# Gate products of the first expert in one timed sequence, and a shorter pause in the gate scaling

## The chip, the cores and the metric

One core of a Trainium2 chip runs the whole program. The metric is the device time of one launch in microseconds (us); lower is better. The core has five engines, each of which takes its instructions strictly in the order in which they are written for it: PE multiplies matrices, DVE (vector), ACT (scalar) and POOL (GpSimd) work on arrays, and SP here only issues DMAs. An engine whose next instruction waits for a semaphore does nothing else meanwhile, even if later instructions could run.

## The reference

Three stages follow one another: an attention with exponential features, a feed-forward layer with squared ReLU, and a mixture of 8 experts over 2304 tokens of width 512. Only the last one concerns us:

```python
logits = x @ w_gate
P = np.exp(logits - logits.max())
for _ in range(8):
    P /= P.sum(1, keepdims=True) + 1e-09
    P /= P.sum(0, keepdims=True) + 1e-09
    P *= N / E
for e in range(E):
    h = np.maximum(x @ w1[e], 0.0)
    out += P[:, e:e + 1] * (h @ w2[e])
```

Every token passes through every expert; `P[:, e]`, the gate of expert e, weighs its result. The eight rounds of scaling need the logits of all tokens, so no gate exists before they are done.

## The kernel before

The expert stage is cut into 16 passes (8 experts, two halves of 512 hidden columns each), and each pass into three groups of 768 tokens, which the code calls pairs (two blocks of 384). The index `n` runs over the 48 combinations; n = 0 to 2 are the first half of expert 0 on pairs 0, 1 and 2, n = 3 to 5 its second half, and n = 6 begins expert 1.

For each n there are two layers, `layer1(n)` and `layer2(n)`. Each is a fast matrix product that does with 7 products (`p1` to `p7` in `SLOTS`) what would take 8 blocks. One such product is 12 matmuls of 128x384. All operands are kept as a high and a low part: ACT casts the high part (L912), DVE subtracts it from the value to get the low part (L913). The results of layer 1 become the operands of layer 2 in `hidden_forms`: POOL forms four differences t1 to t4 (L1205), ACT and DVE split them and three plain blocks. Layer 2 adds its products into `accT` (L1293).

The loop at L1379 interleaves `layer2(n)` with `layer1(n + 1)`, one product of each per step, seven steps per n. Work that fits nowhere in particular is a list of generators, `side`; `tick()` lets the first of them make one move. There are two ticks per step, so 14 per n, and 7 more while `layer1(0)` runs alone. The gate scaling `sinkhorn()` is the first such generator: after the logits it makes `WAIT` empty moves, then eight rounds of four moves, and then puts the gates into DRAM (`prT`, L1159). By the code's count it uses 60 ticks, the last of them the eleventh tick of n = 3.

A gate reaches SBUF by `load_gate` (L1164): 768 gates, repeated on 128 partitions, into one of two buffers of the name `gate`. From expert 1 on it is applied inside layer 1 (L1245). Expert 0 starts before any gate exists, so its sum is multiplied later: `gate_first(q)` loads the gates of pair q and after eight moves multiplies the four rows of `accT` of that pair (L1323), with an empty move after each.

The code's order is not the order on the engines. All instructions pass through a scheduler that runs a model of the program in time and writes down, for each engine, a fixed order; `tc.issue_after` only says what may not come earlier. The expert stage stays on PE in names as follows: `psa` and `psb` are accumulators, `xh` holds weights, `xl` and `hv` the split operands, `w2v` weights of layer 2. The three partial sums that ACT takes out of an accumulator between products (`ma`, `my`, `mu`, L1192) get the next products added by DVE (L1252).

Of the kernel before, what the change touches and what calls it, by code (L numbers as in the profile page):

```python
# [20 lines left out]
def tile_features_attention__moe__sinkhorn_moe(  # L21
# [18 lines left out]
    nc = tc.nc  # L40
# [5 lines left out]
    NE, _, FE = w1.shape  # L46
    KD = DM // P
# [94 lines left out]
    N1 = len(passes)  # L142
    NJ = FE // FB
# [36 lines left out]
    def fetch(p):  # L180

        if p >= NP:
            return
        if p >= N1:
            for w in range(2):
                wf[p, w] = stage(p, w)
                nc.sync.dma_start(wf[p, w], passes[p][w].rearrange("(k p) f -> p k f", p=P))
                yield
            return
        order = [(w, i) for w in range(2) for i in range(KD)]  # L190
        load_raw(p, *order[0])
        for j, (w, i) in enumerate(order):
            if j + 1 < len(order):
                load_raw(p, *order[j + 1])
            decode(p, w, i)
            yield
# [18 lines left out]
    latest = {}  # L215
# [13 lines left out]
    def layer1(p, f, t0, n):  # L229
        wh, wl = wsp[p, 0]  # L230
        ps = pmm.tile([P, 512], F32, tag="mm", name="ps1")
        cs = slice(f * P, (f + 1) * P)
        for kk in range(KD):
            mm3(
                ps[:, :n], wh[:, kk, cs], wl[:, kk, cs],
                xh[:, kk, t0 : t0 + n], xl[:, kk, t0 : t0 + n],
                kk == 0, kk == KD - 1,
            )
        return ps
# [24 lines left out]
    def first_l1(pool, t0, n, fs=range(NFT)):  # L264
        return [split_square(pool, layer1(0, f, t0, n), n, HALF) for f in fs]
# [574 lines left out]
    accT = acc.rearrange("p t d -> p (t d)").rearrange("p (k n) -> p k n", k=KD)  # L840
# [3 lines left out]
    with tc.tile_pool(name="hp1t", bufs=1, reuse_waits="tile") as hpt:  # L844
        g = [ahead + first_l1(hp, *halves[-2], range(len(ahead), NFT)), first_l1(hpt, *halves[-1])]
# [17 lines left out]
    side = []  # L863

    def tick():
        while side:
            try:
                next(side[0])
                return
            except StopIteration:  # L870
                side.pop(0)
# [27 lines left out]


    NB = 384
    WAIT = 20
    NPR = NT // (2 * NB)
    KH = KD // 2
    SLOTS = (("a", "p1", "b11"), ("b", "p5", "t1"), ("a", "p6", "t2"), ("b", "p3", "b22"), ("a", "p7", "t3"), ("b", "p2", "b21"), ("a", "p4", "t4"))
# [70 lines left out]
    order = [(p, q) for p in range(N1, NP) for q in range(NPR)]  # L976

    def split_forms(p, w, dst, temp):

        f = wf.pop((p, w))  # L980

        def a(i, k):
            return f[:, KH * (k - 1) : KH * k, FH * (i - 1) : FH * i]

        s1, s2 = temp(), temp()
        nc.gpsimd.tensor_tensor(s1, a(2, 1), a(2, 2), ALU.add)  # L986
        nc.gpsimd.tensor_tensor(s2, s1, a(1, 1), ALU.subtract)
        nc.gpsimd.tensor_tensor(a(2, 1), a(1, 1), a(2, 1), ALU.subtract)
        of = {"p1": a(1, 1), "p5": s1, "p6": s2, "p3": s2, "p7": a(2, 1), "p2": a(1, 2), "p4": a(2, 2)}
        for i, (_, nm, _) in enumerate(SLOTS):  # L990
            if nm == "p3":
                nc.gpsimd.tensor_tensor(s2, a(1, 2), s2, ALU.subtract)
            split_form(of[nm], dst[i])
            yield
# [57 lines left out]
    for p in range(1, N1):  # L1052
# [10 lines left out]
        for bi, (t0, n) in enumerate(blocks):  # L1063
            g = []
# [46 lines left out]
    def sinkhorn():  # L1111
# [18 lines left out]

        for _ in range(WAIT):
            yield
# [29 lines left out]
    def load_gate(e, q):  # L1162
        g = hp.tile([P, 2, NB], F32, tag="gate", bufs=2, name="gate")
        nc.sync.dma_start(  # L1164
            g.rearrange("p a (t n) -> p (a t) n", n=P),
            prT[2 * NB // P * q : 2 * NB // P * (q + 1), e : e + 1].rearrange("t e n -> e t n").to_broadcast([P, 2 * NB // P, P]),
        )
        return g
# [28 lines left out]
    def hidden_forms(n):  # L1197

        r = hid[n]["r"]
        out = hid[n]["v"] = {}  # L1200
        t = {}

        def diff(nm, x, y):
            t[nm] = sum_tile(nm)
            nc.gpsimd.tensor_tensor(t[nm], x, y, ALU.subtract)  # L1205

        def form(nm, src):
            out[nm] = form_tile()
            split_form(src, out[nm])

        diff("t1", r["12"], r["11"])
        form("b11", r["11"])
        yield
        diff("t2", r["22"], t["t1"])
        form("t1", t["t1"])
        yield
        diff("t3", r["22"], r["12"])
        form("t2", t["t2"])
        yield
        form("b22", r["22"])  # L1220
        diff("t4", r["21"], t["t2"])
        yield
        form("t3", t["t3"])
        yield
        form("b21", r["21"])
        yield
        form("t4", t["t4"])
        yield
# [50 lines left out]
    def layer2(n):  # L1279
        p, q = order[n]  # L1280
        tags = chains(n, "2")
        a = bank(tags["a"])
        b = bank(tags["b"])
        pa_, pb_ = a[:, :, :NB], b[:, :, :NB]
        first = p == N1
        t0 = 2 * NB * q

        def add(i, j, ps, copy=False):
            o = accT[:, KH * (i - 1) : KH * i, t0 + (j - 1) * NB : t0 + j * NB]
            if first and copy:  # L1290
                nc.scalar.copy(o, ps)
            else:
                latest["dve"] = nc.vector.tensor_add(o, ps, o).ins  # L1293

        for i, (ch, nm, fm) in enumerate(SLOTS):
            ps = a if ch == "a" else b
            product(ps, w2v[i], hid[n]["v"][fm], nm in ("p1", "p5", "p2"))
            if nm == "p1":
                add(1, 1, pa_, True)
            elif nm == "p5":  # L1300
                add(2, 2, pb_, True)
            elif nm == "p6":
                add(1, 2, pa_, True)
            elif nm == "p3":
                add(1, 2, pb_)
            elif nm == "p7":
                add(2, 2, pa_)
            elif nm == "p2":
                add(1, 1, pb_)
            else:  # L1310
                add(2, 1, pa_, True)
            yield
        del hid[n]

    def gate_first(q):

        g = load_gate(0, q).rearrange("p a n -> p (a n)")
        for _ in range(8):
            yield
        for c in range(KD):  # L1320
            o = accT[:, c, 2 * NB * q : 2 * NB * (q + 1)]
            with tc.issue_after(latest["dve"]):
                nc.vector.tensor_mul(o, o, g)  # L1323
            yield
            yield

    rows, kept = [], []
# [51 lines left out]
    for n in range(NN):  # L1379
        l2 = layer2(n)  # L1380
        if n + 1 < NN:
            l1 = layer1(n + 1)
            p, q = order[n + 1]
        else:
            l1 = iter(())
            q = None
        if q == 1 and p + 1 < NP:
            weights = fetch(p + 1)
            next(weights)
        elif q == NPR - 1:  # L1390
            next(weights, None)
        w1n = split_forms(p + 1, 0, w1v, sum_weights) if q == NPR - 1 and p + 1 < NP else iter(())
        w2n = split_forms(p, 1, w2v, sum_weights) if q == 0 and p > N1 else iter(())
        nmade = None
        for i in range(NS):
            next(l1, None)
            next(w1n, None)
            if i >= NS - 2 and n + 1 < NN:
                if i == NS - 2:
                    nmade = hidden_forms(n + 1)  # L1400
                next(nmade)
            tick()
            next(l2)
            next(w2n, None)
            if i < 4:
                next(made)
            elif i == NS - 1 and n + 1 < NN:
                next(nmade)
            tick()
            if n == NN - 2 and i >= NS - 4:  # L1410
                square_rows(i - NS + 4)
            if q is None:

                t1 = (NPR - 1) * NRP
                if i < 2:
                    square_rows(4 + i)
                if 1 <= i <= 3:
                    t = NRP + 2 * i - 2
                    finish_rows((t, t + 1), "ab"[i % 2] + "1")
                elif i == NS - 2:  # L1420
                    finish_rows((t1 + NRP // 2, t1 + NRP // 2 + 1), "a1")
        for x in (l1, l2, w1n, w2n):
            for _ in x:
                pass
        made = nmade
        if order[n][0] == N1 + NJ - 1:
            side.append(gate_first(order[n][1]))
    while side:
        tick()
    finish_rows((t1 + NRP - 1, t1), "b1")  # L1430
# [32 lines left out]
```

## Time and profile before

| | us |
|---|---|
| median of 3 runs (2036.91 to 2042.01) | 2039.81 |
| the profiled execution | 2036.81 |
| its span, first to last instruction | 2035.0 |
| PE busy in the span | 2019.3 (99%) |
| DVE busy | 1667.5 (82%) |
| ACT busy | 837.8 (41%) |
| POOL busy | 815.1 (40%) |
| PE stands in the chain that ended last with | 93% |

The profiled execution took 1.8 us more than its span, and 3.0 us less than the median of the timed runs. PE is busy nearly all the time, so a change shows in the time only where PE stands still, or where its granted clock falls. "A tile" in a row is a buffer of the program; `out<-in` says what an instruction writes and reads.

### The profile page before, as it was taken

Reading aid. Unit: us, or ns where it says so; the run is one execution under the profiler, and the core shown is the slowest. Engines: PE = TensorE matmul, PEld = TensorE weight load, DVE = VectorE, ACT = ScalarE, POOL = GpSimd, SP = SyncE. Lnnn points to the kernel's source line nnn. Section 1 sums busy time; section 2 is a strip of 40 time slices with the busy share of each in tenths; the row PEclk is TensorE's granted clock in tenths of the full one; section 3 lists DMA queues with packets and bytes.
Section 4 is the critical chain, followed back from the end, with each engine's and each line's share of the span. In section 5 each row is a group of like instructions: output and inputs, shape, how many; then the busy total and the mean of one; then the engine's idle time right before and its main releaser. Section 6 shows DMA issues by size and latency. Waiting matters only on the chain.

```text
span 2035.0 us, 31524 instructions
## 1 busy us (share of the span) xinstructions
PE 2019.3 (99%) x12528; PEld 1909.2 (94%) x12528; DVE 1667.5 (82%) x1906; ACT 837.8 (41%) x1261; POOL 815.1 (40%) x457
## 2 busy tenths in 40 slices
PE   9999999999999999999999999999999999999999
PEld 5677798888999999999999999999999999999998
DVE  6976338575567989999898989899899898989987
ACT  6777642222335644343343333333333343333332
POOL 4443203241015545344354534544444354534432
PEclk9999999999999999999999999999999999999999
DMA  5454221011246566666777667676767766666664
GB/s 157 127 134 112 66 89 63 31 53 37 114 189 225 202 209 235 211 240 217 251 225 229 211 233 245 219 225 229 223 211 232 252 224 223 216 234 245 203 200 134
DMA packets 192932, 375.14 MB, mean 184 GB/s; under 512 B 84114, under 2 KB 123922, under 8 KB 192786
## 3 DMA queue, kind: packets, MB, share of 16 engines
q1 hardware_dynamic: 192786, 373.13, 55.7%
q8 instruction: 100, 1.64, 0.3%
q14 instruction: 46, 0.38, 0.1%
HBM read 348.67 MB, written 24.34 MB: 183 GB/s over the span
## 4 chain that ended last, share of the span: by engine, by line
PE 93%; DVE 5%; ACT 1%; POOL 1%; DMA 1%; issue 1%; SPq 0%; ACTq 0%; DVEq 0%; POOLq 0%
PE psa L1177 33%; PE psb L1177 32%; PE ps L222 20%; PE psw L222 3%; PE pss L222 3%; DVE acc L1293 1%; PE psg L954 1%; DVE xl L913 1%; DVE dm L102 0%; DVE acc L1323 0%; DVE xh L913 0%; DVE hv L913 0%; POOL eq L102 0%; DMA xl<-xv 0%; DVE r L1245 0%
## 5 line engine op out<-in xcount | busy, mean ns | idle before, releaser
L1177 PE MATMUL psa<-xl,xh 128*128 128x384 f32 x2400 | 446.9, 335 | 3.3 <-DVE xl L913 2.5
L1177 PE MATMUL psb<-xl,xh 128*128 128x384 f32 x2400 | 444.9, 334 | 2.2 <-DVE acc L1293 0.8
L1177 PEld LDWEIGHTS psa<-xl,xh 128*128 128x128 f32 x2400 | 419.7, 188 | 4.2 <-DVE xl L913 2.9
L1177 PEld LDWEIGHTS psb<-xl,xh 128*128 128x128 f32 x2400 | 418.1, 188 | 3.5 <-issue 2.2
L1205 POOL TENSOR_TENSOR t<-r,r 128x768 f32<-128x768 f32 x96 | 207.2, 2158 | 501.4 <-DVE r L1245 455.6
L1205 POOL TENSOR_TENSOR t<-r,t 128x768 f32<-128x768 f32 x96 | 236.3, 2461 | 7.4 <-ACT r L1249 1.9
L913 DVE TENSOR_TENSOR xl<-t,xl 128x768 fp32r<-128x768 f32 x128 | 187.2, 1463 | 1.7 <-ACT xl L912 1.5
L1293 DVE TENSOR_TENSOR acc<-psa,acc 128x768 f32<-128x768 f32 x161 | 153.0, 951 | 38.4 <-PE psa L1177 35.2
L1293 DVE TENSOR_TENSOR acc<-psb,acc 128x768 f32<-128x768 f32 x163 | 155.0, 951 | 33.5 <-PE psb L1177 30.3
L1177 PE MATMUL psa<-xl,w2v 128*128 128x384 f32 x960 | 180.1, 334 | 0.0
L1177 PE MATMUL psb<-xl,w2v 128*128 128x384 f32 x960 | 179.8, 334 | 0.0
L912 ACT CAST xl<-t 128x768 fp32r<-128x768 f32 x128 | 107.2, 838 | 157.4 <-POOL t L1205 66.5
L1177 PEld LDWEIGHTS psa<-xl,w2v 128*128 128x128 f32 x960 | 167.5, 188 | 0.0
L1177 PEld LDWEIGHTS psb<-xl,w2v 128*128 128x128 f32 x960 | 167.4, 188 | 0.0
L912 ACT CAST xl<-r 128x768 fp32r<-128x768 f32 x96 | 80.5, 838 | 161.1 <-PE psb L1177 75.9
L913 DVE TENSOR_TENSOR xl<-r,xl 128x768 fp32r<-128x768 f32 x96 | 133.6, 1392 | 1.6 <-ACT xl L912 1.6
L986 POOL TENSOR_TENSOR s<-wf 128x512 f32<-128x512 f32 x32 | 44.9, 1405 | 214.7 <-DVE xvs L913 80.6
L222 PE MATMUL ps<-xh,w0h 128*128 128x288 f32 (+3 forms) x384 | 130.4, 340 | 0.3 <-ACT r L102 0.2
L222 PE MATMUL ps<-xl,w0h 128*128 128x288 f32 (+3 forms) x384 | 128.8, 335 | 0.0
L222 PE MATMUL ps<-xh,w0l 128*128 128x288 f32 (+3 forms) x384 | 128.5, 335 | 0.0
L222 PE MATMUL ps<-gl,w1h 128*128 128x288 f32 (+3 forms) x384 | 126.9, 336 | 0.0
L222 PE MATMUL ps<-gh,w1l 128*128 128x288 f32 (+3 forms) x384 | 126.2, 335 | 0.0
(209 smaller groups left out, 3568.6 us busy)
## 6 DMA issues: line engine op xcount, KB each, us to landing
xl<-xv SPq DMA_DIRECT2D x329, 768.0 KB, 4.8
wf<-in_moe_w_dram SPq DMA_DIRECT2D x32, 1024.0 KB, 9.8
gate<-prT SPq DMA_DIRECT2D x45, 384.0 KB, 7.7
xv<-xvs SPq DMA_DIRECT2D x14, 768.0 KB, 3.3
raw<-in_moe_w_in_dram SPq DMA_DIRECT2D x16, 512.0 KB, 3.4
raw<-in_moe_w_out_dram SPq DMA_DIRECT2D x16, 512.0 KB
xv<-xl SPq DMA_DIRECT2D x7, 768.0 KB, 3.2
rb<-rden SPq DMA_DIRECT2D x32, 144.0 KB, 3.1
```

The source lines that it names most:

```text
L222: latest["pe"] = op(*args, **how).ins
L912: nc.scalar.copy(v[:, 0], src)
L913: nc.vector.tensor_sub(v[:, 1], src, v[:, 0].bitcast(F32))
L954: ins = nc.tensor.matmul(ps[:, t], accT[:, k, t0 + t * P : t0 + (t + 1) * P], wg[:, k], start=first is None, stop=k == KD - 1, skip_group_ ...
L986: nc.gpsimd.tensor_tensor(s1, a(2, 1), a(2, 2), ALU.add)
L1177: ins = nc.tensor.matmul(ps[:, x, :NB], w[:, wi, k, cs], b[:, bi, k], start=first and k + i == 0, stop=k == KH - 1 and i == 2, skip_group_ ...
L1205: nc.gpsimd.tensor_tensor(t[nm], x, y, ALU.subtract)
L1293: latest["dve"] = nc.vector.tensor_add(o, ps, o).ins
```

## The change

The diff takes 6 from `WAIT`, so each of the eight rounds and the storing of the gates come 6 ticks sooner. By the code's count the scaling now uses 54 ticks, the last of them the fifth of n = 3. `gate_first` becomes one generator for all pairs, which is put into `side` after n = 0 and so starts right behind the scaling, at the sixth tick of n = 3. A table `parts` gives the place of each of the 12 multiplications, a table `loads` that of the loads; the gates of pair 1 are loaded twice.

```diff
-    WAIT = 20
+    WAIT = 14
...
-    def gate_first(q):
-
-        g = load_gate(0, q).rearrange("p a n -> p (a n)")
-        for _ in range(8):
-            yield
-        for c in range(KD):
-            o = accT[:, c, 2 * NB * q : 2 * NB * (q + 1)]
-            with tc.issue_after(latest["dve"]):
-                nc.vector.tensor_mul(o, o, g)
-            yield
+    def gate_first():
+
+        gate = {}
+        loads = {0: 0, 10: 1, 25: 1, 29: 2}
+        parts = {8: (0, 0), 10: (0, 1), 12: (0, 2), 14: (0, 3), 20: (1, 0), 24: (1, 1), 31: (1, 2), 33: (1, 3)}
+        parts.update({37: (2, 0), 40: (2, 1), 43: (2, 2), 46: (2, 3)})
+        for at in range(47):
+            if at in parts:
+                q, c = parts[at]
+                o = accT[:, c, 2 * NB * q : 2 * NB * (q + 1)]
+                with tc.issue_after(latest["dve"]):
+                    nc.vector.tensor_mul(o, o, gate[q])
+            if at in loads:
+                gate[loads[at]] = load_gate(0, loads[at]).rearrange("p a n -> p (a n)")
             yield
...
-        if order[n][0] == N1 + NJ - 1:
-            side.append(gate_first(order[n][1]))
+        if n == 0:
+            side.append(gate_first())
```

The instructions move on all engines, since the scheduler writes every order anew. Three places follow. The multiplication stands at L1323 before and at L1326 now.

**Place A**, the passage from n = 1 to n = 2, on PE. `cs,mean` is the small matmul of a scaling round, the first row with `hv,xh` is the first product of `layer2(2)`. Before:

```order
L1144 MATMUL psa<-cs,mean 128x8
L1177 MATMUL psa<-xl,w2v_6217 128x384 x10
L1177 MATMUL psb<-xl,w2v_6218 128x384 x12
L1177 MATMUL psb<-xl,xh 128x384
L1177 MATMUL psa<-xl,xh 128x384 x12
L1177 MATMUL psb<-xl,xh 128x384 x11
L1177 MATMUL psa<-hv,xh 128x384 x12
```

Now, on the same engine at the same place:

```order
L1144 MATMUL psa<-cs,mean 128x8
L1177 MATMUL psa<-xl,xh 128x384 x12
L1177 MATMUL psa<-hv,xh 128x384 x12
L1144 MATMUL psb<-cs,mean 128x8
L1177 MATMUL psb<-xl,xh 128x384 x12
```

Before, 46 matmuls lie between the small matmul and the first product of `layer2(2)`; now 12 do, and a second small matmul stands between that product and the next.

DVE at place A now (`cr`, `prx`, `rs` and `cs` belong to the scaling; `hv<-r_6848` is the low part that the first product of `layer2(2)` needs, `xl<-t_6852` that of the second):

```order
L1146 RECIPROCAL cr<-psa 128x8
L1147 TENSOR_TENSOR prx<-prx,cr 128x18x8
L1135 TENSOR_REDUCE rs<-prx 128x18
L1136 RECIPROCAL rs<-rs 128x18
L913 TENSOR_TENSOR hv<-r_6848,hv 128x768
L1137 TENSOR_TENSOR prx<-prx,rs 128x18x8
L1139 TENSOR_REDUCE cs<-prx 128x8
L913 TENSOR_TENSOR xl<-t_6852,xl 128x768
```

Before, the same eight steps stand in the same order, with an `xh` split behind the first and an addition to `acc` behind the third.

**Place B**, from n = 3 to n = 4, on DVE now: `tp` is the last step before the gates go to DRAM, `acc<-acc,gate` is the first multiplication, and `mu`, `my` and `ma` are of `layer1(4)`:

```order
L1156 STREAM_TRANSPOSE tp<-pad 128x160
L1293 TENSOR_TENSOR acc<-psb,acc 128x2x384
L1252 TENSOR_TENSOR mu<-psb,mu 128x768
L1326 TENSOR_TENSOR acc<-acc,gate 128x768
L1252 TENSOR_TENSOR my<-psa,my 128x768
L1252 TENSOR_TENSOR ma<-psb,ma 128x768
```

The first multiplication stands three rows behind `tp` and ahead of `my` and `ma` of `layer1(4)`. Before, it stood 15 rows behind `tp`, after the `my` of `layer1(5)`.

PE at place B now, from the last small matmul of the scaling on:

```order
L1144 MATMUL psa<-cs,mean 128x8
L1177 MATMUL psb<-xl,xh 128x384 x12
L1177 MATMUL psb<-xl,w2v_6218 128x384 x12
L1177 MATMUL psa<-xl,xh 128x384 x24
L1177 MATMUL psb<-xl,xh 128x384 x12
L1177 MATMUL psa<-xl,xh 128x384 x12
```

The `x24` are p6 and p7 of `layer1(4)`, which now follow each other directly. The last row is its p4, which adds to the same `psa` that `my<-psa` reads. From the small matmul to p4 lie 60 matmuls, five products.

**Place C**, from n = 4 to n = 5, on DVE now (`hv<-r_7638` and `xl<-t_7642` are the low parts for the first two products of `layer2(5)`):

```order
L1252 TENSOR_TENSOR ma<-psa,ma 128x768
L913 TENSOR_TENSOR xh<-wf_6_7196,xh 128x512
L1293 TENSOR_TENSOR acc<-psb,acc 128x2x384
L913 TENSOR_TENSOR hv<-r_7638,hv 128x768
L1326 TENSOR_TENSOR acc<-acc,gate 128x768
L913 TENSOR_TENSOR xh<-wf_6_7196,xh 128x512
L913 TENSOR_TENSOR xl<-t_7642,xl 128x768
```

Before, a multiplication stood one row ahead of that first low part; now one stands between the two.

## Rows read from the trace of the kernel before

**Rows 1.** Busy time by stretch (us): PE, PEld, DVE, ACT, POOL, granted clock, DMA

```profile
700.00:730.00 30.00, 29.11 (x170) 28.70 (x169) 26.60 (x39) 13.78 (x19) 16.10 (x8) 1.00 0.65 241
...
760.00:790.00 30.00, 29.28 (x169) 28.96 (x168) 27.82 (x26) 15.47 (x22) 14.90 (x8) 1.00 0.68 242
790.00:820.00 30.00, 27.46 (x150) 27.14 (x149) 29.71 (x30) 9.32 (x13) 16.44 (x8) 0.94 0.52 178
...
850.00:880.00 30.00, 29.24 (x169) 28.95 (x168) 29.91 (x31) 11.84 (x17) 15.47 (x8) 1.00 0.63 213
...
910.00:1500.00 590.00, 590.00 (x3405) 589.82 (x3404) 531.91 (x520) 219.94 (x297) 270.57 (x134) 1.00 0.69 230
```

**Rows 2.** Timeline of PE: start, us, what, count, idle time before and its releaser

```profile
814.32 5.83 PE L1177 MATMUL psa<-xl,xh 128*128 128x384 f32 x23 [2.54 <-DVE xl L913]
```

**Rows 3.** Busy time by stretch, three us of the same place

```profile
815.00:818.00 3.00, 3.00 (x12) 3.00 (x11) 3.00 (x4) 0.41 (x1) 2.38 (x1) 0.52 0.20 53
```

**Rows 4.** Timeline of PE at place A

```profile
682.80 0.28 PE L1144 MATMUL psa<-cs,mean 128*128 128x8 f32 x2
...
691.00 2.24 PE L1177 MATMUL psa<-hv,xh 128*128 128x384 f32 x12
693.08 1.20 PE L1177 MATMUL psb<-xl,xh 128*128 128x384 f32 x6
```

**Rows 5.** Timeline of DVE at place A

```profile
684.55 0.19 DVE L1146 RECIPROCAL cr<-psa 128x8 f32<-128x8 f32 x1
...
685.22 0.30 DVE L1147 TENSOR_TENSOR prx<-prx,cr 128x144 f32<-128x144 f32 x1
685.55 0.32 DVE L1135 TENSOR_REDUCE rs<-prx 128x18 f32<-128x162 f32 x1
...
686.66 0.26 DVE L1136 RECIPROCAL rs<-rs 128x18 f32<-128x18 f32 x1
686.83 1.42 DVE L913 TENSOR_TENSOR hv<-r,hv 128x768 fp32r<-128x768 f32 x1
688.17 1.96 DVE L1137 TENSOR_TENSOR prx<-prx,rs 128x144 f32<-128x144 f32 x1
690.16 0.45 DVE L1139 TENSOR_REDUCE cs<-prx 128x8 f32<-128x152 f32 x1
690.52 4.65 DVE L913 TENSOR_TENSOR xl<-t,xl 128x768 fp32r<-128x768 f32 x2
```

**Rows 6.** Timeline of POOL, first and last of four at place C

```profile
775.09 2.22 POOL L1205 TENSOR_TENSOR t<-r,r 128x768 f32<-128x768 f32 x1 [6.43 <-ACT r L1249]
...
782.31 2.30 POOL L1205 TENSOR_TENSOR t<-r,t 128x768 f32<-128x768 f32 x1
```

**Rows 7.** Timeline of DVE at place C

```profile
776.39 1.74 DVE L1323 TENSOR_TENSOR acc<-acc,gate 128x768 f32<-128x768 f32 x1
778.05 2.61 DVE L913 TENSOR_TENSOR hv<-r,hv 128x768 fp32r<-128x768 f32 x1
...
782.83 2.60 DVE L913 TENSOR_TENSOR xl<-t,xl 128x768 fp32r<-128x768 f32 x1
```

**Rows 8.** Timeline of SP (DMA issues), the gates to DRAM and back

```profile
753.23 1.76 SPq L1159 DMA_DIRECT2D prT<-tp  x4
...
756.18 0.97 SPq L1164 DMA_DIRECT2D gate<-prT  x2
```

**Rows 9.** Line L1164, issue to landing

```profile
DMA to landing us min/median/max: 7.3/7.7/9.0
```

**Rows 10.** Timeline of DVE, the last step of the scaling and the first multiplication

```profile
752.87 0.33 DVE L1156 STREAM_TRANSPOSE tp<-pad 128x160 f32<-128x160 f32 x1
...
770.27 0.94 DVE L1323 TENSOR_TENSOR acc<-acc,gate 128x768 f32<-128x768 f32 x1
```

**Rows 11.** Line L1192: duration in ns, min/median/max, first and last start

```profile
L1192 ACT COPY mu<-psa x24: 791/802/802, 619.7 to 1961.6; 128x768 f32<-128x768 f32 x24
```

**Rows 12.** Timeline of DVE from n = 5 to n = 6

```profile
807.57 1.96 DVE L1323 TENSOR_TENSOR acc<-acc,gate 128x768 f32<-128x768 f32 x1
```

## The prediction

> **What bounds the kernel now.** I read the busy times by stretch first. PE is busy in every microsecond from 910 to 1500 us; in the four stretches of 30 us around the passages that the change touches it stands still for 0.89, 0.72, 2.54 and 0.76 us, 30 less its busy time [rows 1]. These 4.9 us, and what the clock does after them, are all that can be won there. DVE is the engine next to the limit: 27.82, 29.71 and 29.91 us busy of 30 in three of these stretches [rows 1]. So what makes DVE wait in its queue there is hardly caught up before PE notices.
>
> The timeline of PE came next. The longest wait, 2.54 us, ends with a low part from DVE, and the 23 matmuls behind it last 5.83 us [rows 2]. Twelve take 2.24, and the next product starts 2.08 after them [rows 4], so one takes 0.173 and 23 would take 4.15: the wait is followed by 1.68 us of slow matmuls. The granted clock there is 0.52, hence mostly the lower of its two levels, 1.2 instead of 2.4 GHz [rows 3]. The wait cost 4.2 us in all.
>
> The timeline of DVE shows what makes such a low part late. An operation of DVE with both inputs in SBUF takes 0.94 us alone [rows 10] and 1.74 to 2.61 while POOL forms its four differences [rows 6, 7, 12]. POOL's run from the first to the last of these lasts from 775.09 to 784.61. The rows fit turns: one instruction of POOL, one of DVE.
>
> **The change part by part.** What is added is small: 12 multiplications before and after, one load of gates more. The six pauses less cost nothing in themselves. What counts is where the scheduler has put things.
>
> *Place A.* I count from the end of the small matmul. DVE runs cr (0.19), prx, rs (0.32), the second reciprocal (0.26), and then the low part hv [rows 5]. The first prx took 0.30, since POOL had not begun, the second 1.96. Now `my` stands two rows ahead of cr, and the ACT steps that follow from it start POOL at about the time of prx, so I take 1.96 for the first one too, and 2.0 for hv (1.42 here, 2.61 at most [rows 5, 7]). Sum 4.7 us. PE has only p4 to do (2.08) and the one matmul with the high part (0.17), and p4 itself must wait until cr has read `psa`, about 0.4. It needs hv at 2.65 and waits 2.1. The other 11 matmuls end at 6.6; the small matmul behind them needs the second prx (1.96) and cs (0.45), at 7.1: 0.5 more. The next product needs the low part of t1, half of the 4.65 later [rows 5], at 9.4, and PE is there at 7.4: 2.0. Together 0.4 + 2.1 + 0.5 + 2.0 = 5.0 at the upper end. Before, 46 matmuls covered all this: hv was done at 688.25 and needed at 691.17, the first xl at 692.85 and needed at 693.25 [rows 4, 5]. If POOL comes late, with prx at 0.30 and hv at 1.42, hv is no wait and 0.4 + 0.3 + 2.0 = 2.7 remain; if PE itself comes later than by the model, 0. I take 4.7, near the upper end, because `my` stands so close ahead.
>
> *Place B.* The first multiplication now stands three rows behind tp. Ahead of tp there are one full addition (0.9), cr (0.19), prx (0.30), the copy (no row; like prx 0.3) and tp (0.33): 2.0 from the last small matmul. From the first store of the gates to the issue of the load took 756.18 - 753.23 = 2.95 [rows 8], the store starting 0.03 after tp [rows 10]. The load lands after 7.7, at best 7.3, at worst 9.0 [rows 9]. Then the multiplication and `my`, 0.9 each [rows 10]: 2.0 + 3.0 + 7.7 + 1.8 = 14.5. DVE does nothing between, since it works in order; behind the multiplication are queued `my`, `ma` and all low parts of n = 4. PE has five products (10.4), and p7 waits for ACT's copy of p6's sum, 0.80 [rows 11] and some 0.2 to hand over, which is a wait of 1.0 by itself. It wants to start p4 at 11.4 and waits until 14.5: 3.1, with the bounds of the load 2.7 to 4.4. One load of a form between tp and the stores would add 0.4, so I take 3.4. With the 1.0 the place costs 4.4, and 1.7 for the clock after it, by the one wait of this size in the trace [rows 2, 3]. Before, the same load had 14 us, from 756.18 to 770.27, and nobody waited [rows 8, 10].
> The Trainium skill ("DMA: Bandwidth & Descriptors", the section on the anatomy of one DMA on the SWDGE path) gives a fit of 2.0 us plus the bytes by 436 GB/s; for the 384 KB of this load that is an estimate of 2.9 us, and place B would then cost only the 1.0. The trace disagrees, with 7.3 as the shortest of 45 such loads [rows 9], and the measurement decides.
>
> *Place C.* A multiplication stands between the low parts of b11 and t1, while POOL is at its differences; one such operation more or less ahead of t1 is 2.6 us [rows 7]. Before, one stood ahead of both and PE waited 0.72 [rows 1]. The count of operations is the same, so 0.72 is one bound; but DVE comes here late from place B and has 2.2 us of 30 to spare, so the other is 0.72 + 2.6 = 3.3. I take 3.0, which is 2.3 more than before, and 1.0 for the clock, which may or may not fall.
>
> *What is won.* From n = 5 to 6 one multiplication of 1.96 us [rows 12] no longer stands ahead of the low part on which PE waited 2.54. About 0.6 would be left, or 1.1 if the multiplication now ahead of t1 makes that late: 1.4 less, and the 1.7 of the clock with it, 3.1. The multiplications after 846 us are gone too, and with them the 0.76 [rows 1].
>
> *What costs nothing.* The gate loads move past the loads of forms on SP. A form is loaded four products of layer 1 ahead of its use, with four of layer 2 between: 8 x 2.08 = 16.6 us. A gate load that waits for a multiplication one or two steps of 4.2 us away leaves half of that. Were that cover gone, PE would wait for the form, some 4 us each time. The load of pair 1's gates that is made twice adds one of 46.
>
> **The sum.** 4.7 (A) + 6.1 (B with its clock) + 3.3 (C) - 3.1 - 0.8 = +10.2 us on the profiled 2036.81, 2047.0. That execution was 3.0 under the median of the timed runs; on that median it makes 2050.0. With all low ends (A 0, B 1.0 + 2.7 without the clock, C 0, all of 2.54 + 1.68 and 0.76 won) it is -1.3, with all high ends (A 5.0, B 5.4 and C 2.6, each with 1.7 of clock, 1.4 won) +16.7.
>
> **The rivals.** *A is covered*, if POOL and PE come some microseconds otherwise than I order them. For it: before, both low parts were ready in time, the one by 2.9 us and the other by 0.4 [rows 4, 5]. Against it: 34 matmuls of cover are gone. 10.2 - 4.7 = +5.5, 2045.3.
>
> *The gates are there in time.* If the load took 3 us, B costs 1.0, no clock falls, and C keeps its old 0.72: 4.7 + 1.0 - 3.1 - 0.8 = +1.8, 2041.6. Against it stands every one of the 45 loads. The page of the Trainium skill named above would have it so.
>
> *Faster.* The multiplications leave the passages in which POOL and DVE take turns with PE waiting, n = 5 to 7, for places where DVE has room, and all waits in the four stretches go with the fall of the clock: 4.9 + 1.7 = 6.6 less, 2033.2. It decides at place B: the multiplication must find its gates landed, so that `my` is read before PE comes to p4. For it: the 2.54 us are the largest wait of the stage, and a multiplication is among its causes. Against it: 14.5 us against 11.4.
>
> **Chances.** Forecast 0.71, A covered 0.13, gates in time 0.10, faster 0.06 (no room for more is seen). A measurement of this kernel can tell about 0.3%, 6.1 us, from no change. Of the forecast some 0.66 lies above that, of A covered half: slower 0.72, same 0.22, faster 0.06. The range goes from 2041, below which are the faster case and part of the case of early gates, to 2057, the high ends.
>
> **What would show it.** At place B in the new profile, DVE stands idle for some 5 us until a gate load ends its wait at L1326, and PE then waits about 3 to 4 us on `my` at L1252. At place A PE waits two or three times within 8 us, on hv (L913), cs (L1139) and xl (L913). At place C it waits up to 3 us on xl (L913). The 2.54 us from n = 5 to 6 are halved, and the granted clock falls at B. I am wrong if the first multiplication starts without an idle DVE ahead of it, or if PE's idle time from 680 to 900 us is under 8 us.

## The result and the profile after

The changed kernel takes 2050.18 us (median of 5 runs, 2048.24 to 2050.5) where the kernel before takes 2039.81: a ratio of 1.0053, with a 95% interval of 1.0042 to 1.0064, so it is slower, clear of the noise but by half a percent only: 10.4 us between the medians. The profiled execution took 2048.93, with a span of 2047.1 against 2035.0.

First the busy times by stretch, after, to set beside [rows 1] (columns as there):

```profile
670.00:700.00 30.00, 26.18 (x149) 25.23 (x148) 27.31 (x40) 16.35 (x23) 14.50 (x8) 1.00 0.59 211
700.00:730.00 30.00, 29.71 (x164) 29.39 (x164) 23.32 (x34) 15.01 (x21) 12.66 (x7) 0.95 0.57 194
730.00:760.00 30.00, 24.80 (x142) 23.94 (x141) 16.74 (x29) 6.49 (x8) 1.85 (x1) 0.96 0.48 155
760.00:790.00 30.00, 27.57 (x144) 27.61 (x145) 22.98 (x24) 14.86 (x20) 13.61 (x8) 0.87 0.70 216
790.00:820.00 30.00, 29.66 (x171) 29.34 (x170) 29.04 (x28) 13.69 (x19) 16.58 (x8) 1.00 0.77 252
820.00:850.00 30.00, 28.90 (x167) 28.58 (x167) 28.73 (x31) 9.31 (x12) 8.38 (x4) 1.00 0.78 247
910.00:1500.00 590.00, 590.00 (x3406) 590.00 (x3405) 533.53 (x518) 220.13 (x297) 273.87 (x135) 1.00 0.69 227
```

PE stands still (30 less its busy time) for 3.82 us before 700 and for 5.20 and 2.43 us around 760; from 910 on it is busy all the time, as before. Next the timeline of PE, where a number in brackets at a row's end is the idle time before it and what ended it. The rows in the order of places A (four), B (three), C (one), and the passage from n = 5 to 6:

```profile
690.32 2.35 PE L1177 MATMUL psa<-xl,xh 128*128 128x384 f32 x12 [0.30 <-DVE cr L1146]
694.82 2.19 PE L1177 MATMUL psa<-hv,xh 128*128 128x384 f32 x11 [1.98 <-DVE hv L913]
697.26 0.36 PE L1144 MATMUL psb<-cs,mean 128*128 128x8 f32 x2 [0.25 <-DVE cs L1139]
699.19 3.36 PE L1177 MATMUL psb<-xl,xh 128*128 128x384 f32 x11 [1.30 <-DVE xl L913]
...
704.85 2.24 PE L1177 MATMUL psb<-xl,xh 128*128 128x384 f32 x12
...
751.25 2.35 PE L1177 MATMUL psa<-xl,xh 128*128 128x384 f32 x12 [0.89 <-ACT mu L1192]
...
762.43 4.18 PE L1177 MATMUL psa<-xl,xh 128*128 128x384 f32 x12 [6.74 <-DMA xl<-xv]
...
769.29 4.33 PE L1177 MATMUL psa<-xl,xh 128*128 128x384 f32 x24
...
803.09 4.43 PE L1177 MATMUL psa<-xl,xh 128*128 128x384 f32 x24 [0.34 <-DVE acc L1293]
...
834.62 3.40 PE L1177 MATMUL psb<-xl,xh 128*128 128x384 f32 x18 [1.10 <-DVE xl L913]
```

The long wait is at p4 of `layer1(4)`, where it was forecast, but it is twice as long, and it was ended by a DMA: `xl<-xv`, the load of a form. (A form is the ready-made operand of one product of layer 1; SP loads it from DRAM, at L1006, into one of four buffers.) The price of slow matmuls is taken from starts, at 0.1733 us for each at the higher clock. From 762.43 to 769.29 there are 24, 6.86 us where 24 x 0.1733 = 4.16 would do: 2.7 us of lower clock. From 699.19 to 704.85 there are 23, 5.66 for 3.99: 1.7. The granted clock of these two stretches of 30 us is 0.87 and 0.95.

Now SP at place B (start, us for the issues, what; these rows answer [rows 8]), and then two pieces of the chain of waits:

```profile
746.23 0.32 SPq L1006 DMA_DIRECT2D xl<-xv  x1
746.60 1.86 SPq L1159 DMA_DIRECT2D prT<-tp  x4
751.38 0.38 SPq L1164 DMA_DIRECT2D gate<-prT  x1
751.81 0.54 SPq L1006 DMA_DIRECT2D xl<-xv  x1
752.39 3.50 SPq L1164 DMA_DIRECT2D gate<-prT  x1
```

```profile
748.02 3.21 DMA prT<-tp
...
751.81 10.48 DMA xl<-xv
```

SP stands at the gate load until the stores have landed, and the form that PE needs at 755.69 (762.43 - 6.74) is queued behind it. Issued at 751.81, it lands after 10.48 us; the median of such a load is 4.5 (the last number of this row):

```profile
xl<-xv SPq DMA_DIRECT2D x329, 768.0 KB, 4.5
```

DVE at the same place, to set beside [rows 10], shows what the prediction had looked for:

```profile
758.79 0.96 DVE L1326 TENSOR_TENSOR acc<-acc,gate 128x768 f32<-128x768 f32 x1 [6.60 <-DMA gate<-prT]
759.66 0.95 DVE L1252 TENSOR_TENSOR my<-psa,my 128x768 f32<-128x768 f32 x1
```

DVE does stand idle for its gates, 6.60 us, and `my` ends at 760.61, 4.9 us after PE wanted p4. So two things hold PE, and the form, at 762.29, comes last by 1.7 us. Without experiments the profile's word for the releaser (the DMA) and the prediction's (`my`) can't be weighed against each other: either would have held PE.

### The profile page after: what moved, and what is told of

It is laid out like the page before. It is cut to its first block, busy times and chain, and to the rows that moved or that the text cites. A ratio compares the mean times of both kernels' runs of the same rounds, so it can differ in the third digit from the quotient of the medians.

```text
span 2047.1 us, 31524 instructions
## 1 busy us (share of the span) xinstructions
PE 2022.7 (99%) x12528; PEld 1911.8 (93%) x12528; DVE 1656.7 (81%) x1906; ACT 837.1 (41%) x1261; POOL 812.9 (40%) x457
## 4 chain that ended last, share of the span: by engine, by line
PE 93%; DVE 3%; DMA 2%; ACT 1%; POOL 1%; issue 0%; SPq 0%; ACTq 0%; POOLq 0%; DVEq 0%
PE psb L1177 33%; PE psa L1177 33%; PE ps L222 19%; PE psw L222 3%; PE pss L222 3%; DMA xl<-xv 1%; PE psg L954 1%; DVE dm L102 0%; DVE xl L913 0%; DMA gate<-prT 0%; POOL eq L102 0%; DVE acc L1326 0%; DVE acc L1293 0%; PE pskt L222 0%; DVE wf L102 0%
## 5 line engine op out<-in xcount | busy, mean ns | idle before, releaser
L1293 DVE TENSOR_TENSOR acc<-psb,acc 128x768 f32<-128x768 f32 x163 | 154.8, 950 | 39.6 <-PE psb L1177 36.5
L1293 DVE TENSOR_TENSOR acc<-psa,acc 128x768 f32<-128x768 f32 x161 | 152.8, 949 | 36.6 <-PE psa L1177 33.3
```

## The experiments

All ratios are to the kernel before, with 95% intervals.

**1. The sequence without the shorter pause.** In the changed kernel:

```diff
-    WAIT = 14
+    WAIT = 20
```

> The new sequence with the old pause of 20 moves. The theory of the prediction: place A belongs to the pause alone, and place B too (with the old pause the gates are stored and loaded as before, a form of SP goes ahead of the load, and the first multiplication stands behind my and ma). So A and B vanish, of the old waits 0.30 and 0.59 stay, the one of 0.72 stays, the one of 2.54 with its 1.7 us of slow matmuls falls below 1.2, the one of 0.76 goes: idle time of PE from 680 to 900 us under 3.5 us, time 3 to 5 us below the kernel before (ratio near 0.998). Rival: the sequence of places is itself at fault; then the time stays above the kernel before, by some 4 us or more.

Measured: 2040.93 us, 1.0006 (0.9997 to 1.0015): the same time as before, where 3 to 5 us less were expected. PE:

```profile
721.42 2.53 PE L1177 MATMUL psb<-xl,xh 128*128 128x384 f32 x13 [0.30 <-DVE cr L1146]
724.53 2.19 PE L1177 MATMUL psb<-xl,xh 128*128 128x384 f32 x11 [0.59 <-DVE xl L913]
774.72 2.32 PE L1177 MATMUL psa<-xl,xh 128*128 128x384 f32 x12 [1.55 <-DMA xl<-xv]
...
837.40 2.32 PE L1177 MATMUL psb<-hv,w2v 128*128 128x384 f32 x12 [1.17 <-DVE acc L1293]
848.91 5.82 PE L1177 MATMUL psb<-xl,xh 128*128 128x384 f32 x23 [2.77 <-DVE xl L913]
```

A is gone and so is the long wait of B, so both came with the pause. The wait of 2.54 is gone too, but new waits of 1.55, 1.17 and 2.77 stand at other places, with 1.7 us of slow matmuls behind the last. Behind the last two the chain has a gate load of layer 1 that landed 11.47 us after its issue, with DVE waiting 5.66 us for it:

```profile
823.52 11.47 DMA gate<-prT
```

```profile
835.43 0.96 DVE L1245 SCALAR_TENSOR_TENSOR r<-mu,gate 128x768 f32<-128x768 f32 x1 [5.66 <-DMA gate<-prT]
```

**2. The shorter pause without the sequence.** In the kernel before:

```diff
-    WAIT = 20
+    WAIT = 14
```

> The kernel before with the pause of 14 moves alone; the multiplications stay in their old generator and stand on DVE behind my and ma at place B, while SP keeps the order stores, gate load, form. A shows as in the changed kernel (about 3.8 us of waits and 1.5 of slow matmuls). For B two theories. The prediction's: PE waits there on the multiplication that waits for its gates; then here only the 0.89 on the copy and at most 1.3 on my are left, and the time is before + 6 to 8. The rival: PE waits there on the form (the xl tile) that SP could issue only behind the wait for the stores and the gate load; then the 6.7 us and the 2.9 of slow matmuls are here too, and with the old waits of 0.72 and 2.54 kept the time is before + 13 to 16, not below the changed kernel.

Measured: 2053.37 us, 1.0067 (1.0055 to 1.008), by the median 13.3 us over before, at the low end of the 13 to 16 that the theory of the form gave. Place A shows the same four waits (0.30, 1.98, 0.25, 1.29); at place B and from n = 5 to 6:

```profile
763.33 4.18 PE L1177 MATMUL psa<-xl,xh 128*128 128x384 f32 x12 [6.13 <-DMA xl<-xv]
...
832.13 5.82 PE L1177 MATMUL psa<-xl,xh 128*128 128x384 f32 x23 [2.53 <-DVE xl L913]
```

Here no multiplication stands ahead of `my`, and PE waits at the same product nearly as long. This speaks for the form. The pause by itself costs all of the change's loss and more. By the medians the sequence takes back about 3 us; the intervals of the two ratios overlap, but the wait of 2.53 with its slow matmuls, which the change has no more, is in the trace.

**3 to 5. Form and multiplication, each alone.** In the third kernel the multiplications of pair 0 come later (the first of the two edits below, on the changed kernel). In the fifth each gate load stands behind a form on SP (the second edit), which also parts the first two gate loads: the second is issued at 752.39 in the change, at 767.42 in run 5 and at 760.37 in run 4. The fourth has both edits.

```diff
-        parts = {8: (0, 0), 10: (0, 1), 12: (0, 2), 14: (0, 3), 20: (1, 0), ...
+        parts = {14: (0, 0), 15: (0, 1), 16: (0, 2), 18: (0, 3), 20: (1, 0), ...
```

```diff
-                nc.sync.dma_start(x.bitcast(F32), xv[order[m][1], i])
+                latest["form"] = nc.sync.dma_start(x.bitcast(F32), xv[order[m][1], i]).ins
...
-                gate[loads[at]] = load_gate(0, loads[at]).rearrange("p a n -> p (a n)")
+                with tc.issue_after(latest["form"]):
+                    gate[loads[at]] = load_gate(0, loads[at]).rearrange("p a n -> p (a n)")
```

> The changed kernel with the four multiplications of pair 0 later (places 14, 15, 16, 18 for 8, 10, 12, 14), behind my and ma; SP's order at place B is unchanged. Prediction's theory: the DVE no longer stands idle for 6.6 us, PE's wait of 6.7 falls to 1.3 or less and the slow matmuls after it go: some 8 us below the changed kernel, near 2041. Rival (the form): PE still waits some 6.5 us for the xl tile, released by the DMA, and the time stays within 2 us of the changed kernel.

> As the run with the multiplications of pair 0 later, and besides the first gate load stands behind one more form on SP. Prediction's theory: no difference to that run. Rival (the form): the form is issued right behind the stores, near 748.5, and lands before PE wants it at 755.7, so the wait of 6.7 and its slow matmuls go here and not there: 8 to 9 us below that run. If both causes stand beside each other in the changed kernel, it takes both edits to lose the wait, and this run is the first without it.

> The changed kernel, each gate load behind the form last written ahead of it, the multiplications at the places of the change. At place B one form now goes ahead of the first load, and on DVE my stands ahead of the multiplication, ma still behind it; at place C the order on DVE is that of the change. The gates should land 8 to 9 us after an issue at 751.6, so ma ends near 762. Theory that form and multiplication each hold PE in the changed kernel, the form longer: PE is now held by ma instead, one product later than before, from 757.8 on, for some 4 us and 1.7 of slow matmuls: 2 to 5 us below the changed kernel. Theory that the form alone holds it: no such wait, and the time of the run with form first and late multiplications, near 2044.5. Place C: if the forecast of 3.0 us was only hidden by the form's delay, PE waits there 2 us or more on xl; if PE and DVE leave place B together whatever holds them, under 1 us.

| | multiplication early | late |
|---|---|---|
| gate load ahead of the form | the change: 1.0053 (1.0042 to 1.0064) | run 3: 1.0048 (1.0036 to 1.0061) |
| form ahead of the gate load | run 5: 1.0047 (1.0034 to 1.006) | run 4: 1.0021 (1.0012 to 1.003) |

The longest wait of PE at place B, in runs 3, 4 and 5:

```profile
763.49 4.18 PE L1177 MATMUL psa<-xl,xh 128*128 128x384 f32 x12 [7.89 <-DMA xl<-xv]
```

```profile
763.04 5.79 PE L1177 MATMUL psa<-xl,xh 128*128 128x384 f32 x23 [2.90 <-ACT xl L912]
```

```profile
762.81 4.21 PE L1177 MATMUL psb<-xl,xh 128*128 128x384 f32 x12 [5.26 <-DVE ma L1252]
...
803.12 4.44 PE L1177 MATMUL psa<-xl,xh 128*128 128x384 f32 x24 [2.07 <-DVE acc L1293]
```

Either edit alone leaves the time where it is; only both together lower it. Run 3 came out as the theory of the form had it, not 8 us lower; run 5 missed the 2 to 5 us below the change that were expected of it. So form and multiplication each hold PE, side by side. With the multiplication out of the way PE waits 7.89 us for the form; with the form in time it waits 5.26 us, one product later, for `ma` behind the multiplication.

Run 4 also tells how much of the hold is SP's standing still. Its SP, and the start of p4 on its PE:

```profile
750.52 0.34 SPq L1006 DMA_DIRECT2D xl<-xv  x1
751.56 0.38 SPq L1164 DMA_DIRECT2D gate<-prT  x1
```

```profile
755.65 2.24 PE L1177 MATMUL psa<-xl,xh 128*128 128x384 f32 x12
```

The form can't go before 750.5 even here: SP waits 1.8 us for PE, which must first be done with the buffer. It then lands in 4.4 us, 0.7 us before p4 starts. In the change it was issued 1.3 us later (751.81) and took 6.1 us longer (10.48): 1.3 + 6.1 - 0.7 = 6.7, the whole wait. So most of it is the slow transfer behind the gate load, and only 1.3 us is the standing still of SP. In run 5 the order is turned around, and now it is the gate load that takes longer, 9.89 us instead of 7.4 in the change:

```profile
751.01 9.89 DMA gate<-prT
```

Run 4 lies 4.9 us below run 3 by the medians, where 8 to 9 were expected. With nothing else late, PE runs into ACT's split of a difference that POOL has only just formed: 2.90 us, with 1.6 of slow matmuls behind it (23 in 5.79 us, for 4.15). The chain of waits of run 4 ahead of it:

```profile
759.70 2.40 POOL t L1205
...
762.13 0.84 ACT xl L912
```

This third wait was hidden behind the other two. The clock also fell at place A in run 4's profiled execution (11 matmuls in 3.89 us, in run 3 in 2.19).

Run 5 settles place C. DVE has there the order of the change, and nearly its times: the low part of t1 starts at 799.61, in the change at 799.57 (its row):

```profile
799.57 2.59 DVE L913 TENSOR_TENSOR xl<-t,xl 128x768 fp32r<-128x768 f32 x1
```

PE comes at 801.05 (803.12 - 2.07) in run 5 and at 802.75 (803.09 - 0.34) in the change. What PE waits for in both is the addition `acc` (L1293), which stands behind that low part on DVE. What the form adds to the wait at B, PE doesn't wait for at C, and so run 5 gains nothing.

**6 and 7. Better places with the old pause.** Both keep `WAIT = 20`. Run 6 (the first diff, on the changed kernel) puts the multiplications closer together, loads each gate once, and has the gate loads behind forms as in run 5. Run 7 (the second) has other tables only, with the multiplications of pairs 1 and 2 and their loads 6 places sooner, and those of pair 0 by up to 2:

```diff
-        loads = {0: 0, 10: 1, 25: 1, 29: 2}
-        parts = {8: (0, 0), 10: (0, 1), 12: (0, 2), 14: (0, 3), 20: (1, 0), 24: (1, 1), 31: (1, 2), 33: (1, 3)}
+        loads = {0: 0, 10: 1, 24: 2}
+        parts = {8: (0, 0), 9: (0, 1), 10: (0, 2), 11: (0, 3), 20: (1, 0), 21: (1, 1), 22: (1, 2), 23: (1, 3), 33: (2, 0), 35: (2, 1), 37: (2, 2), 39: (2, 3)}
```

```diff
+        loads = {0: 0, 4: 1, 19: 1, 23: 2}
+        parts = {8: (0, 0), 9: (0, 1), 10: (0, 2), 12: (0, 3), 14: (1, 0), 18: (1, 1), 25: (1, 2), 27: (1, 3), 31: (2, 0), 34: (2, 1), 37: (2, 2), 40: (2, 3)}
```

> A try at a better version: the old pause of 20, one sequence whose multiplications stand at 8 to 11, 20 to 23 and 33, 35, 37, 39, each gate loaded once and behind the form last written ahead of it. No place A, a form ahead of the first two gate loads, and the buffer of a gate is free before layer 1 of expert 1 loads its own. Expected: of PE's waits 0.3 and 0.6 from the scaling, 1.2 or less from n = 5 to 6, nothing else over 1 us, no slow matmuls: 4 to 5 us below the kernel before. If loads and multiplications in one sequence collide whatever their places, there is a wait for a DMA (of PE for xl or of DVE for a gate) of over 1.5 us, and no gain.

> The sequence with the old pause of 20 and most places 4 to 6 earlier, so that the later multiplications stand about where the change has them in time. In the run with the old pause alone a gate load of layer 1 landed 11.5 us after its issue, DVE stood idle for 5.7 us at L1245 and PE for 1.2 and 2.8 us. Theory: that load came late because its buffer was held by the multiplications of pair 1; then these waits (4.0 us and 1.7 of slow matmuls) go here, while the wait of 1.5 us on a form behind two adjacent gate loads stays, and the time is 3 to 5 us below that run. Rival: the load is slow whatever its place, because forms stand ahead of it in the transfers; then DVE waits 4 us or more for a gate again.

Measured: 2034.49 us, 0.9981 (0.9972 to 0.9989), and 2034.84 us, 0.9981 (0.9972 to 0.999); both are some 4 us faster than before, and they can't be told apart. For run 6 that is at the low end of what was expected (4 to 5 us). What PE waits for beside the 0.30 and 0.59 of the scaling, in run 6 and in run 7:

```profile
820.79 3.76 PE L1177 MATMUL psb<-xl,xh 128*128 128x384 f32 x20 [1.51 <-DVE xl L913]
```

```profile
774.26 2.32 PE L1177 MATMUL psa<-xl,xh 128*128 128x384 f32 x12 [0.99 <-DMA xl<-xv]
820.38 3.39 PE L1177 MATMUL psb<-xl,xh 128*128 128x384 f32 x18 [1.07 <-DVE xl L913]
```

Run 6 has one wait over the 1.2 us that were expected, 1.51. In run 7 the waits of 1.17 and 2.77 of run 1 are gone, and 5 us with them by the ratios, as the theory of the held buffer has it. It moved the whole sequence, though, so why that load took 11.47 us after its issue is not told by it. The wait on a form behind two adjacent gate loads stays, at 0.99 us.

## Why the prediction was right, and where it was not

The time came out at 2050.18 where 2050.0 was forecast. That the two lie so close is luck: four terms of the sum were off by 0.9 to 4.2 us, and nearly cancel. B was 4.2 too small and the clock at A, 1.7, was left out; C was 3.7 too large and the waits at A 0.9. The direction, the waits at A and their places, the place of the wait at B with one of its two causes, and the gain from n = 5 to 6 were foreseen. In the profile of the change against that of before:

| step | forecast | measured | from |
|---|---|---|---|
| A, waits | +4.7 | +3.8 | 0.30 + 1.98 + 0.25 + 1.30 |
| A, clock | 0 | +1.7 | 23 matmuls |
| B, waits | +4.4 | +7.6 | 0.89 + 6.74 |
| B, clock | +1.7 | +2.7 | 24 matmuls |
| C | +3.3 | -0.4 | 0.34 - 0.72 |
| n = 5 to 6 | -3.1 | -3.0 | 1.10 + 0.1 - 2.54 - 1.7 |
| the wait of 0.76 | -0.8 | -0.8 | gone |
| waits of the scaling, 0.30 and 0.59, from 719 us on | none | -0.6 | 0.29 is left |
| sum | +10.2 | +11.0 | the spans differ by 12.1 |

1.1 us of the difference in spans is in none of these terms. Of it 0.7 is a longer wait of PE for a load (`wphi`, 0.9 against 0.2) in the attention stage, which the edit doesn't touch; the rest stays unassigned.

**A** is right in kind, each of its four waits in its place, and 0.9 too large; run 1 shows that it belongs to the pause. That the clock falls behind it was not counted. With the same waits (0.30, 1.98, 0.25 and 1.30) the 11 matmuls at its end took 3.36 us in the change and 2.18 in run 2, so the waits alone don't settle whether it falls.

**B** failed in the step "What costs nothing", where the gate loads were let past the loads of forms on SP with 16.6 us of cover. The cover was taken from the program, eight products between a form's load and its use. On PE at place B it isn't there. The buffer of p4's form was p6's before, and between p6 and p4 PE has only p7 and p2 (the second half of the `x24` and the `x12` behind it in PE's order at place B) and the wait of 0.89: 5.1 us from 750.52 to 755.65 in run 4, where nothing on SP stands ahead. That is enough for a landing of 4.4 us, but not for one of 10.48 that is issued 1.3 us later. The Trainium skill ("DMA: Bandwidth & Descriptors", the section on queues, rings and completion order) says that a queue's descriptors are taken up in the order of its ring on each DMA engine. The traces agree: the form behind the gate load took 10.48 us here and 11.54 in run 3, ahead of it 4.4 (run 4), and the gate load behind a form took 9.89 (run 5). What the second gate load, right behind the form, adds to this wasn't tested by itself. The prediction's own term for the multiplication was too small as well. Its steps were 2.0 to `tp`, 2.95 from the first store to the load, 7.7 for the load; measured were 2.0, then 0.6 until the stores, 4.78 (751.38 - 746.60) and 7.4 (758.79 - 751.38). The stores were slower because a form was issued just ahead of them; that is argued from the order, not tested. Without the form, the multiplication would have held PE until `my` was done, 4.9 us instead of 3.4. Run 5 shows a hold of that kind with 5.26, though of `ma`, one product later, and behind a gate load that was itself slower.

**C** failed in "DVE comes here late from place B". DVE came late, but PE came later still, since the wait and the slow clock at B were both longer than forecast, and in the change DVE even waits for PE ahead of place C:

```profile
790.29 0.96 DVE L1252 TENSOR_TENSOR ma<-psa,ma 128x768 f32<-128x768 f32 x1 [0.21 <-PE psa L1177]
...
792.38 0.96 DVE L1293 TENSOR_TENSOR acc<-psb,acc 128x768 f32<-128x768 f32 x1 [0.53 <-PE psb L1177]
```

With the form in time the wait is there, 2.07 us in run 5. It was part of the forecast that B held PE by way of DVE alone; under a hold that PE feels more than DVE, the term had to go. The low part `xl`, which the forecast named, is also not what PE waits for there, but the addition behind it.

**What is won** from n = 5 to 6 was right to 0.1 us, and run 2, which keeps the wait of 2.53, shows that it is the sequence's doing.

Of the rivals, "A is covered" fell with the four waits and "the gates are there in time" with the 7.4 us. The faster case named the right point, that `my` must not stand behind a multiplication that waits for its gates. That alone isn't enough with the shorter pause: run 4 has it and still loses at place A and to ACT's split. Runs 6 and 7, with the old pause, are that case, at some 4 us below the kernel before.

## What to carry to other kernels

When a step that issues DMAs is moved, follow the queue it is issued on: what stands behind a DMA that waits for a semaphore is not issued (1.3 us here), and what is issued behind a slow transfer lands late (6.1 us here). Count the cover of a load in the engine's own order, from the instruction that frees its buffer to the one that needs it, not in the program. When two things hold an engine at one place, taking away either shows nothing, so undo them one at a time and together before a cost is put down to one of them. And a wait forecast for a later place holds only as long as the two engines leave the earlier one with the distance that was assumed.

## What the runs showed of the hardware that was not expected

The issue of a second gate load right behind a first and a form held SP for 3.50 us in the change, 3.60 in run 2 and 3.69 in run 3, where an issue takes 0.38 (SP's rows of the change). A load of a form behind one gate load took 10.48 and 11.54 us, ahead of it 4.4. Nearly the same pattern of waits at place A was followed by a fall of the clock in the change and in runs 4 and 5 (the last 11 matmuls in 3.36, 3.89 and 2.87 us) and not in runs 2 and 3 (2.18 and 2.19); why is open.
